# Chunk minimum and maximum by halving steps, and the bounds' product on GpSimd, in a sparse-attention and soft-MoE kernel

## Chip, cores and metric

The kernel runs on one core of a Trainium2 chip. The metric is the device time of one execution in microseconds (us). The engines are TensorE (PE; PEld is its weight load), VectorE (DVE), ScalarE (ACT) and GpSimd (POOL). Each works through its own instructions in program order and waits for others through semaphores. Here POOL also issues every load, and SyncE (SP) issues the stores of the output.

## What is computed

```
# q, k, v: 4 batches x 8 heads x 768 positions x 64, f32
k_min, k_max = min, max of k over each chunk of 32 positions     # 24 chunks
ub   = sum over d of max(q * k_min, q * k_max)                   # bound, per position and chunk
ub   = ub where the chunk is not in the future, else -1e9
top  = the 6 chunks of the largest ub, for each position
attn = softmax(q k^T / 8, over the positions in top, causal) @ v
# soft MoE over x = attn as 3072 rows x 512
logits = x @ phi                                                 # 32 slots
slots  = softmax(logits over rows)^T @ x
y      = relu(slots @ w1[e]) @ w2[e]                             # 8 experts, 4 slots each
out    = softmax(logits over slots) @ y                          # 3072 x 512, f32
```

## The kernel before

The work goes by pairs of heads: 16 pairs, two heads of 64 on the 128 partitions. The program is written out by hand, as a loop `for i in range(-2, 16)` (L469) that is a software pipeline. In round i the scores, the exponentials and the causal masks of pair i are made. For pair i+1 the bounds are made (`ubound`) and the six best chunks are picked (`select`, `ns_transposes`, `evac_ns`). For pair i+2 the keys and queries are transposed and prepared (`transposes`, `evac_T`, `kmin`, `kmax`, `qsplit`). For pair i-1 the product with v is made (`pv`), and pair i-2 is normalised and transposed. The loads of pair i+4 are issued. Four pairs make a batch, so in two of every four rounds MoE steps of a batch come between (`moe_logits` and `moe_copy` in one, `moe_max` to `moe_ct` in the next); the others are plain rounds. Ahead of the loop stands a preamble (L138 to L175): on GpSimd the loads of pairs 0 to 2, of v 0 and 1, of one weight tile and of phi, with mask building between them; on VectorE memsets.

Each engine takes its instructions in the order in which the program issues them, so a step's place in a round is its place in five queues. For GpSimd a round's order is: the masks of scores 0 and 1 (L291, an affine select on e_sb of 128x256), a small cast (L244, into ns_t), the k and q loads (L127), the masks of scores 2 and 3, the v load (L132), a weight load in most rounds (L120), and the masks of scores 4 and 5. For VectorE it is: normalise (inv L320, x_sb L321), the twelve MAX8 (L242), the comparison (ns_t L245), kmin (L202), the copy of xT (L341), kmax (L208) and bd (L210), the copy of nsT (L261), and the two qpn (L218, L219).

The lines that the change touches are these. `kmin` reduces kT (128 x 768, bf16, 24 chunks of 32) to 24 minima, in the tile mm; `kmax` writes the maxima beside them, and then multiplies mm by headsel, a 0/1 mask that keeps each head's rows, into bd (2 x 2 x 24 a partition). In the next round `ubound` reads bd and qpn on TensorE, so that a PSUM tile ub_ps holds the bounds, which MAX8 reads.

The score tiles in PSUM (p_sc) are two, so the scores of a group wait until the exponential two groups before has read its tile. nsT is needed by the mask matmul of the scores (L277). The e_sb tiles are nine.

Of the kernel before, what the change touches and what calls it, by code (L numbers as in the profile page):

```python
# [11 lines left out]
BF16 = mybir.dt.bfloat16  # L12
ALU = mybir.AluOpType
ACT = mybir.ActivationFunctionType
AX = mybir.AxisListType
# [3 lines left out]
CH = 32  # L19
NCHUNK = 24  # L20
NQT = 6
P = 128
# [24 lines left out]
def kernel(  # L47
# [10 lines left out]
    nc = tc.nc  # L58
# [45 lines left out]
    i_ctx, u_ctx, l_ctx = ExitStack(), ExitStack(), ExitStack()  # L104
# [2 lines left out]
    ep = i_ctx.enter_context(tc.tile_pool(name="ep", bufs=9, side="right"))  # L107
    ep5 = i_ctx.enter_context(tc.tile_pool(name="ep5", bufs=2, side="right"))
    tpu = u_ctx.enter_context(tc.tile_pool(name="tpu", bufs=2, side="right"))
    inp = l_ctx.enter_context(tc.tile_pool(name="inp", bufs=3, side="right"))  # L110

    def load_w(i):
# [35 lines left out]
    for h in range(2):  # L148
# [3 lines left out]
        out=qgrp, in_=qgrp, compare_op=ALU.not_equal, fill=1.0, base=0,  # L152
# [3 lines left out]
        out=caus[:4], in_=caus[:4], compare_op=ALU.is_ge, fill=NEG, base=0,  # L156
# [5 lines left out]
    for h in range(2):  # L162
        sl = schunk[h * 64:(h + 1) * 64]
        nc.gpsimd.affine_select(
            out=sl, in_=sl, compare_op=ALU.not_equal, fill=NEG, base=0,
# [3 lines left out]
            out=sl, in_=sl, compare_op=ALU.not_equal, fill=-1.0, base=-NCHUNK,  # L169
# [20 lines left out]
    def evac_T(i, nm):  # L190
# [5 lines left out]
        )  # L196
        st[nm + "T", i] = t

    def kmin(i):
        kT = st["kT", i].rearrange("d (c x) -> d c x", x=CH)  # L200
        mm = tpu.tile([P, 2, 1, NCHUNK], BF16, name="mm", tag="mm")
        nc.vector.tensor_reduce(mm[:, 0, 0, :], kT, axis=AX.X, op=ALU.min)  # L202
        st["mm", i] = mm

    def kmax(i):
        kT = st["kT", i].rearrange("d (c x) -> d c x", x=CH)
        mm = st.pop(("mm", i))
        nc.vector.tensor_reduce(mm[:, 1, 0, :], kT, axis=AX.X, op=ALU.max)  # L208
        bd = tpu.tile([P, 2, 2, NCHUNK], BF16, name="bd", tag="bd")
        nc.vector.tensor_tensor(  # L210
            bd, mm.broadcast_to([P, 2, 2, NCHUNK]), headsel.broadcast_to([P, 2, 2, NCHUNK]), op=ALU.mult,
        )
        st["bd", i] = bd
# [255 lines left out]
    for i in range(-2, NPAIR):  # L469
# [38 lines left out]
        if have(i + 2):  # L508
            transposes(i + 2, "q")
            evac_T(i + 2, "q")  # L510
            kmin(i + 2)
        if have(i - 2):
            evac_x(i - 2)
        if have(i + 2):
            kmax(i + 2)
# [58 lines left out]
    op = ctx.enter_context(tc.tile_pool(name="op", bufs=5))  # L574
# [87 lines left out]
    for m in range(B * NQT // 2):  # L662
        o_sb = op.tile([P, 2, Dm], F32, name="o_sb", tag="o_sb")
        rows = out[m * 2 * P:(m + 1) * 2 * P, :].rearrange("(p x) d -> p x d", x=2)
        for x in range(2):
            pool, tag = homes[n % 5]
# [41 lines left out]
```

## Time and profile before

| | us |
|---|---|
| median of 3 runs (177.87 to 177.99) | 177.93 |
| the profiled execution | 177.53 |
| its span, first to last instruction | 175.8 |
| the reductions L202 and L208, 16 each | 15.2 and 15.1 |
| the products L210, 16 | 4.7 |
| the casts L244 on POOL, 16 | 3.7 |

The span is shorter than the execution, which holds some start and end around it. A timeline line gives the start in the span, the duration, the engine, the line of the source, the operation, the output and input tiles with their sizes, the count, and in brackets the idle time ahead of it with what ended that. The chain of work that ended last is followed back from the last instruction, at each step to what released it; a line gives start, duration and the work. Matmuls overlap in a pipeline, and so do neighbouring VectorE instructions by some 0.08 us where one doesn't need the other, so durations can add up to more than the time between two starts.

### The profile page before, as it was taken

How to read it: one execution, taken by the hardware profiler on the slowest of the kernel's cores; microseconds unless marked ns; L12 is line 12 of the kernel's file. 1: busy time of each engine (PE TensorE's matmuls, PEld its weight loads, DVE VectorE, ACT ScalarE, POOL GpSimd, SP SyncE). 2: the span in 40 equal slices, each digit the busy share in tenths (PEclk: the TensorE clock that was granted, in tenths of full speed). 3: DMA queues.
4: the chain of work that ended last, by engine and by line, in shares of the span. 5: the costliest groups of instructions: out<-in, count | busy, mean ns of one | idle time of the engine just before them, and what ended most of it. 6: DMA issues, size and time to landing. Idle time of an engine off the chain costs nothing.

```text
span 175.8 us, 5994 instructions
## 1 busy us (share of the span) xinstructions
PE 139.1 (79%) x2486; PEld 95.9 (55%) x2486; DVE 128.8 (73%) x429; ACT 120.0 (68%) x163; POOL 99.9 (57%) x194
## 2 busy tenths in 40 slices
PE   0449888999889889999988999999689569986500
PEld 0334556777567657766765776677467444532000
DVE  4456979999889998999998999999752650246530
ACT  2336798989789778988977698897667321156430
POOL 7995679869768557877775585759344600000000
PEclk9999999999999999999999999999999956999755
DMA  3999999999999999999999999199999993009995
GB/s 50 167 158 180 194 206 200 206 197 209 179 212 193 215 185 143 200 172 203 172 147 203 169 207 141 17 187 211 200 214 214 213 215 72 4 13 403 402 405 212
DMA packets 40460, 32.92 MB, mean 187 GB/s; under 512 B 26353, under 2 KB 34545, under 8 KB 40433
## 3 DMA queue, kind: packets, MB, share of 16 engines
q0 software_dynamic: 38416, 26.25, 101.8%
q1 hardware_dynamic: 2016, 6.29, 9.1%
q8 instruction: 19, 0.31, 0.7%
q14 instruction: 9, 0.07, 0.1%
HBM read 52.49 MB, written 6.29 MB: 334 GB/s over the span
## 4 chain that ended last, share of the span: by engine, by line
PE 36%; ACT 19%; DVE 13%; DMA 12%; POOL 11%; issue 5%; POOLq 0%; DVEq 0%; ACTq 0%
ACT e_sb L289 13%; DMA k_in<-in_k_dram 7%; PE sc_ps L271 6%; DMA out_dram<-o_sb 5%; PE at_ps L308 5%; PE sc_ps L277 4%; PE tr_ps L184 3%; PE h_ps L605 3%; DVE x_sb L321 3%; POOL e_sb L291 3%; POOL q_in L127 2%; PE ns_ps L253 2%; POOL k_in L127 2%; PE so_ps L640 2%; PE si_ps L427 2%
## 5 line engine op out<-in xcount | busy, mean ns | idle before, releaser
L289 ACT ACTIVATE e_sb<-sc_ps 128x1024 bf16<-128x1024 f32 x96 | 83.6, 936 | 10.9 <-PE sc_ps L277 9.9
L291 POOL TENSOR_SCALAR_AFFINE_SELECT e_sb<-e_sb 128x256 bf16<-128x256 bf16 x96 | 39.5, 423 | 32.7 <-ACT e_sb L289 32.0
L271 PE MATMUL sc_ps<-qT,kT 64*128 64x512 bf16 (+3 forms) x256 | 39.6, 310 | 6.6 <-ACT e_sb L289 6.3
L277 PE MATMUL sc_ps<-nsT,smask 64*128 64x512 bf16 (+3 forms) x256 | 36.8, 306 | 0.0
L308 PE MATMUL at_ps<-v_t,e_sb 128*128 128x65 bf16 x672 | 29.4, 194 | 1.2 <-DVE x_sb L321 1.1
L308 PEld LDWEIGHTS <-e_sb 128*128 128x128 bf16 x672 | 25.1, 98 | 3.4 <-DVE x_sb L321 1.6
L271 PEld LDWEIGHTS <-kT 64*128 64x128 bf16 x256 | 15.8, 94 | 16.8 <-issue 8.7
L242 DVE MAX8 mx<-ub_ps 128x8 f32<-128x24 f32 x192 | 18.8, 170 | 4.6 <-PE ub_ps L231 4.5
L202 DVE TENSOR_REDUCE mm<-kT 128x24 bf16<-128x768 bf16 x16 | 15.2, 949 | 4.0 <-ACT kT L193 4.0
L132 POOL DMA_DIRECT2D v_t<-in_v_dram x16 | 16.7, 1042 | 1.9 <-PE ns_ps L253 1.2
L193 ACT COPY kT<-tr_ps 128x768 bf16<-128x768 bf16 x16 | 12.8, 803 | 6.5 <-PE tr_ps L184 6.5
L321 DVE TENSOR_TENSOR x_sb<-at_ps,inv 128x768 bf16<-128x768 f32 (+2 forms) x17 | 15.5, 910 | 0.6
L277 PEld LDWEIGHTS <-smask 64*128 64x128 bf16 x256 | 13.1, 95 | 4.4 <-issue 0.3
L208 DVE TENSOR_REDUCE mm<-kT 128x24 bf16<-128x768 bf16 x16 | 15.1, 942 | 0.0
L193 ACT COPY qT<-tr_ps 128x768 bf16<-128x768 bf16 x16 | 13.2, 825 | 2.7 <-PE tr_ps L184 2.7
L184 PE MATMUL tr_ps<-ident,k_in 128*64 128x128 bf16 x192 | 9.2, 237 | 6.6 <-DMA k_in<-in_k_dram 5.5
L670 DVE TENSOR_SCALAR o_sb<-o_ps,cinv 128x512 f32<-128x512 f32 x12 | 8.6, 748 | 7.2 <-PE o_ps L668 4.1
L231 PE MATMUL ub_ps<-bd,qpn 128*128 128x48 bf16 x192 | 10.4, 187 | 2.8 <-DVE qpn L218 2.5
L127 POOL DMA_DIRECT2D k_in<-in_k_dram x16 | 11.7, 729 | 1.3 <-POOLq L692 0.8
L261 DVE COPY nsT<-ns_ps 128x768 bf16<-128x768 bf16 x16 | 8.9, 556 | 4.0 <-PE ns_ps L253 3.5
L672 ACT ACTIVATE o_sb<-o_ps,cinv 128x512 f32<-128x512 f32 x12 | 7.8, 688 | 5.7 <-DMA out_dram<-o_sb 3.8
L127 POOL DMA_DIRECT2D q_in<-in_q_dram x16 | 11.5, 721 | 0.0
(95 smaller groups left out, 213.2 us busy)
## 6 DMA issues: line engine op xcount, KB each, us to landing
w_sb<-in_moe_w_dram POOLq DMA_DIRECT2D x16, 1024.0 KB, 12.9
out_dram<-o_sb SPq DMA_DIRECT2D x10, 512.0 KB, 5.5
k_in<-in_k_dram POOLq DMA_DIRECT2D x16, 192.0 KB, 7.9
q_in<-in_q_dram POOLq DMA_DIRECT2D x16, 192.0 KB, 8.1
v_t<-in_v_dram POOLq DMA_DIRECT2D x16, 192.0 KB, 9.3
out_dram<-o_sb SPq DMA_DIRECT2D x4, 256.0 KB, 3.4
phi_sb<-in_moe_phi_dram POOLq DMA_DIRECT2D x1, 32.0 KB, 9.6
```

The source lines that it names most:

```text
L127: nc.gpsimd.dma_start(out=t, in_=src.rearrange("h (p g) d -> p h (g d)", p=P))
L132: nc.gpsimd.dma_start(out=v_t[i % NV][:, :, :, :D], in_=v[b, 2 * j:2 * j + 2].rearrange("h (g p) d -> p h g d", p=P),)
L193: nc.scalar.copy(t.rearrange("d (p g) -> d p g", g=NQT), st.pop((nm + "ps", i)).rearrange("d g p -> d p g"),)
L202: nc.vector.tensor_reduce(mm[:, 0, 0, :], kT, axis=AX.X, op=ALU.min)
L208: nc.vector.tensor_reduce(mm[:, 1, 0, :], kT, axis=AX.X, op=ALU.max)
L242: nc.vector.max(mx[:, a, :], ub[:, a, :])
L271: nc.tensor.matmul(ps[:, h, c:c + w], lhsT=kT[r, kg * P:(kg + 1) * P], rhs=qT[r, qs], start=True, stop=False,)
L277: nc.tensor.matmul(ps[:, h, c:c + w], lhsT=smask[r, kg].rearrange("p a b -> p (a b)"), rhs=nsT[r, qs], start=False, stop=True,)
L289: nc.scalar.activation(e[:, :, :w], st.pop(("scps", i, g))[:, :, :w], func=ACT.Exp, scale=scale)
L291: nc.gpsimd.affine_select(out=e[:, :, :P], in_=e[:, :, :P], compare_op=ALU.is_ge, fill=0.0, base=0, pattern=[[0, 2], [1, P]], channel_mult ...
L308: nc.tensor.matmul(o, lhsT=st["e", i, g][:, h, c:c + P], rhs=v_t[i % NV][:, h, kg, :], start=(kg == 0), stop=(kg == t),)
L321: nc.vector.tensor_tensor(st["x", b][:, t0:t1, 2 * j:2 * j + 2, :].rearrange("p t h d -> p h t d"), at[:, :, :, :D], inv.broadcast_to([P, ...
```

## The change

The two reductions over 32 elements become three steps each: the elementwise minimum (or maximum) of the first 16 and the last 16 of each chunk, of the first 8 and the last 8 of that, and a reduction over 8. Two tiles of one buffer each, from a new pool, hold what lies between. The product bd goes from VectorE to GpSimd, in the same place of the program.

```diff
+    tpf = u_ctx.enter_context(tc.tile_pool(name="tpf", bufs=1, side="right"))
...
+    def fold(out, kT, op):
+        a = tpf.tile([P, NCHUNK, CH // 2], BF16, name="fold_a", tag="fold_a")
+        nc.vector.tensor_tensor(a, kT[:, :, :CH // 2], kT[:, :, CH // 2:], op=op)
+        b = tpf.tile([P, NCHUNK, CH // 4], BF16, name="fold_b", tag="fold_b")
+        nc.vector.tensor_tensor(b, a[:, :, :CH // 4], a[:, :, CH // 4:], op=op)
+        nc.vector.tensor_reduce(out, b, axis=AX.X, op=op)
+
     def kmin(i):
...
-        nc.vector.tensor_reduce(mm[:, 0, 0, :], kT, axis=AX.X, op=ALU.min)
+        fold(mm[:, 0, 0, :], kT, ALU.min)
         st["mm", i] = mm
 
     def kmax(i):
...
-        nc.vector.tensor_reduce(mm[:, 1, 0, :], kT, axis=AX.X, op=ALU.max)
+        fold(mm[:, 1, 0, :], kT, ALU.max)
         bd = tpu.tile([P, 2, 2, NCHUNK], BF16, name="bd", tag="bd")
-        nc.vector.tensor_tensor(
+        nc.gpsimd.tensor_tensor(
             bd, mm.broadcast_to([P, 2, 2, NCHUNK]), headsel.broadcast_to([P, 2, 2, NCHUNK]), op=ALU.mult,
         )
```

In the built order VectorE has 48 instructions more (two tensor_tensor for each of 32 folds, less 16 products), and GpSimd 16 more; each product stands on GpSimd where it stood in the program, which for pairs 0 and 1 is behind the whole preamble and ahead of the first cast, or behind the loads of round -1. The orders of TensorE and ScalarE are the same.

## The prediction

> **What bounds the kernel now.** I read the page's busy shares first: no engine fills the span.
>
> ```profile
> span 175.8 us, 5994 instructions
> PE 139.1 (79%) x2486; PEld 95.9 (55%) x2486; DVE 128.8 (73%) x429; ACT 120.0 (68%) x163; POOL 99.9 (57%) x194
> ```
>
> So each stage has its own limit, and three stages matter here. Next came the chain that ended last, in order of time; this is its part for the start:
>
> ```profile
> 12.46 0.29 POOL identf masks.py:199
> 13.00 0.83 PE ns_ps L253 x6
> 13.85 0.56 DVE nsT L261
> 14.41 0.86 DVE mm L202
> 15.27 0.87 DVE mm L208
> 16.16 0.26 DVE bd L210
> ```
>
> Up to 12.75 us POOL works through its preamble (loads, masks), and the first work behind it sets the pace. Then VectorE is on the chain, with the very instructions that are changed. The timeline of the same stretch shows why POOL stands there:
>
> ```profile
> 8.46 0.26 DVE L210 TENSOR_TENSOR bd<-mm,headsel 128x96 bf16<-128x96 bf16 x1
> 9.22 0.22 PE L231 MATMUL ub_ps<-bd,qpn 128*128 128x48 bf16 x1 [2.34 <-DVE qpn L218]
> 10.50 1.17 DVE L242 MAX8 mx<-ub_ps 128x8 f32<-128x24 f32 x12 [0.92 <-PE ub_ps L231]
> 12.46 0.29 POOL masks.py:199 TENSOR_SCALAR_AFFINE_SELECT identf<-identf 128x128 f32<-128x128 f32 x1
> 12.71 0.23 POOL L244 CAST ns_t<-mx 128x12 bf16<-128x12 f32 x1
> 13.00 0.82 PE L253 MATMUL ns_ps<-ident,ns_t 128*128 128x128 bf16 x6 [1.75 <-POOL ns_t L244]
> ```
>
> Today bd, the ub matmuls, MAX8 and the comparison of pair 0 (done at 12.17) run beside POOL's preamble. Only the small cast queues behind it.
>
> Third, the timeline of a plain round (no MoE step), 83.46 minus 76.61 = 6.85 us long:
>
> ```profile
> 80.59 0.26 DVE L210 TENSOR_TENSOR bd<-mm,headsel 128x96 bf16<-128x96 bf16 x1
> 81.76 0.39 PE L271 MATMUL sc_ps<-qT,kT 64*128 64x512 bf16 x2 [0.19 <-ACT e_sb L289]
> 82.47 1.94 ACT L289 ACTIVATE e_sb<-sc_ps 128x1024 bf16<-128x1024 f32 x2 [0.48 <-PE sc_ps L277]
> 83.46 1.17 DVE L242 MAX8 mx<-ub_ps 128x8 f32<-128x24 f32 x12 [0.25 <-PE ub_ps L231]
> ```
>
> ScalarE is idle 0.48 us a round, because the next scores wait for a score buffer that its own exponential frees: it closes its own ring of 6.85 us. VectorE's only gap in the round is the 0.25 before MAX8, so it works through 6.6 of the 6.85: room, but little.
>
> **The change, part by part.**
>
> *Start.* In the built order of the changed kernel POOL's preamble stays ahead of the loop, so bd(0) becomes the instruction right behind identf, ahead of the cast. It can't start before 12.71. Its price is in no row: POOL's one-input selects take 0.41 us for 256 elements and 0.29 for 128, so about 0.17 fixed and 0.94 ns an element; 96 elements are 0.26 with one input. Ends: 0.23 (the cast of 12 elements) and 0.53 (two whole one-input passes). I take 0.35 (fixed part once, elements twice). Then bd ends at 13.06, and the ub matmuls start 0.06 later (cast end to ns_ps is that today). From the last wait in ub today (9.64) to MAX8 (10.50) is 0.86; with the two matmuls ahead, MAX8 starts at 14.03. MAX8 to the end of the comparison is 1.67 today (12.17 minus 10.50): 15.70. The cast runs inside that (needs MAX8, 15.2). So ns_ps starts at 15.76 instead of 13.00: **+2.76 us**, since bd, ub, MAX8 and the comparison no longer run beside the preamble but after it.
>
> The Trainium skill ("GPSIMD Engine Reference", section 4.1, Engine selection) speaks against this half of the edit: two-input elementwise work belongs on VectorE, GpSimd being about two times slower. By its 2.6 cycles an element at 1.2 GHz an estimate is 0.21 us for 96 elements, 0.38 with the trace's fixed 0.17, and the sum would grow by 0.03. It speaks of the engine's rate, and nothing of the place in its queue.
>
> *The fold, uncontended.* tensor_reduce: 768 elements 0.945, 192 elements (rm L411) 0.344: 0.144 fixed and 1.04 ns an element. tensor_tensor in f32: 32 elements 0.184, 192 elements 0.358: 0.15 fixed, 1.09 ns an element. Whether bf16 halving runs at two elements a step no row shows for this operation; the bf16 copy L261 does 768 in 0.556, so 0.52 ns an element beside a fixed 0.15, and this nearest row says yes. Then 384 outputs are 0.35, 192 are 0.25, the last reduce 0.34; two dependent starts add 0.04 each (kmax end 80.55, bd 80.59): 1.02 against 0.945, **+0.08** a fold. At one element a step: 0.56 + 0.36 + 0.34 + 0.08 = 1.34, +0.40. At the start two folds of pair 1 are on the chain (+0.16), less bd (0.18 to the next start) = about 0; but bd(1) on POOL comes behind the qpn pair or in between: -0.1 to +0.26. I take **+0.1**.
>
> *Locks in the loop.* These rows decide the rest:
>
> ```profile
> 21.03 0.78 POOL L291 TENSOR_SCALAR_AFFINE_SELECT e_sb<-e_sb 128x256 bf16<-128x256 bf16 x2
> 21.29 0.65 DVE L210 TENSOR_TENSOR bd<-mm,headsel 128x96 bf16<-128x96 bf16 x1
> ...
> 96.84 1.02 POOL L132 DMA_DIRECT2D v_t<-in_v_dram  x1
> 97.60 0.36 DVE L413 TENSOR_TENSOR lc<-lg,rm 128x192 f32<-128x192 f32 x1
> ```
>
> bd takes 0.26 alone and 0.65 under two selects: it ended 0.13 after the second. lc takes its free 0.36 under a DMA issue. So the fold's tensor_tensors will wait for selects, not for issues. qpn does wait for issues: L219 took 0.87 us at 88.50 instead of 0.34, until the v_t issue ended at 89.21.
>
> In a plain round kmin meets the k and q issues (free), kmax meets the selects of scores 2 and 3 (79.56 to 79.99, 80.16 to 80.57). Stepping through: kmax's first half ends at 80.19, its second at 80.71, the reduce at 81.09; nsT starts at 81.04 (80.91 before), ends at 81.60; its first reader, the mask matmul L277, runs at 81.98. Hidden. bd on POOL 81.13 to 81.48; qpn 81.48 to 82.1; x_sb as before: no bd, no late MAX8. **Loop: 0**, with 0.1 to 0.2 us of cover; once it is gone, each excess tenth costs a tenth per round. v_t is issued 0.8 later; behind it stand the w_sb issue and the selects of scores 4 and 5, read a round later, and POOL is level again by the next k issue.
>
> *Given back.* In round 4 the k load comes late:
>
> ```profile
> 45.80 0.53 PE L184 MATMUL tr_ps<-ident,k_in 128*64 128x128 bf16 x12 [0.65 <-DMA k_in<-in_k_dram]
> ```
>
> The round takes 7.80 us by its exponentials (44.26 to 52.06), 0.95 over a plain one. The load was issued 12.5 us earlier into a full queue. All that follows the start moves 2.9 us later, the DMA queue hardly: by 19.9 us 2.87 MB of 3.02 MB issued have moved, so it is not dry when the delayed w_sb 1 comes. The wait goes: **-0.95** (0 to -0.95). In round 1 both qpn waited for issues (0.75 and 0.80 us) on the chain: **-0.3** (0 to -0.4) as v_t comes later.
>
> *Sum.* 177.53 (the profiled execution; its span 175.8 and 1.7 around it) + 2.76 + 0.1 + 0 - 0.95 - 0.3 = 179.14. The median of the runs, 177.93, is 0.40 above the profiled one: **179.5**.
>
> **Rivals.**
>
> *The loop becomes VectorE's* (27%). If v_t's issue takes the port between the two qpn, the second waits as at 88.50: +0.5, 0.4 beyond the cover, in some 8 plain rounds: +3.2, 182.7. For it: 50.88 and 88.02, where v_t began 0.1 to 0.2 ahead of qpn. Against: v_t wants the port 0.39 after its start (1.19 and 1.07 instead of 1.02 fit this), and behind a bd of 0.35 the second qpn is in by then. It decides when bd is shorter than 0.3 us or the folds run 0.2 over my sum. Range 180.4 to 184.
>
> *No doubled rate* (7%). Folds at 1.34: 0.64 more a round, 0.55 beyond the cover, 13 rounds: +7, 186.6. A code load ahead of POOL's first tensor_tensor would land here too; the built order shows none added.
>
> *Not slower* (10%): the loop was VectorE's already, and ScalarE only followed. Then a round loses bd (0.32) and qpn's usual 0.1 of waiting, and pays 0.16: -0.26, times 13 is -3.4 against +1.6: 176.1. VectorE's 6.6 of 6.85 speak for it, ScalarE's wait for its own buffer against. It decides when plain rounds fall under 6.72 us; half as much gives about 178. I split it 7 faster, 3 the same.
>
> *The start partly hidden* (4%): 178.3 to 179.0.
>
> **The numbers.** Forecast 179.5 (179.0 to 180.4): 52%. From 178.3 to 183.2 are the forecast, the partly hidden start and most of the first rival: 8 in 10. The measurement tells 0.2% (0.36 us) from no change: faster 7%, the same 4%, slower 89%.
>
> **What would show it.** bd(0) on POOL at 12.71, ns_ps(0) near 15.8; plain rounds still 6.85; no DMA wait in round 4; kmax's halves stretched under selects; bd on POOL 0.35. I am wrong if ns_ps(0) stays near 13, if plain rounds leave 6.85 by over 0.1, or if the first half takes 0.55 alone.

## The result, and the profile after

The changed kernel takes 178.86 us (177.98 to 180.07), the kernel before, run beside it, 177.18 us (176.21 to 177.99), medians of 17 runs each. The ratio is 1.0105, with a 95% interval of 1.0081 to 1.0129 (it is worked out from the single runs, so it is not quite the quotient of the medians, 1.0095): **slower by about 1%**. The forecast was 179.5 (178.3 to 183.2); 178.86 lies in that range, but just under the 179.0 to 180.4 that the prediction gave to its main path. The profiled execution of the changed kernel took 179.98 us (span 178.2), 2.45 more than that of before; it is among the slowest of its 17, so I use the traces for where the time went, and the medians for how much it is.

Lines below the change stand eight lines lower: the scores are L279 and L285, the masks L299, nsT L269, MAX8 L250. Those above it stand one lower: v_t is L133. The new lines are L202, L204 and L205 (the fold), L218 (bd on POOL), L226 and L227 (qpn). First the busy shares of the page of after:

```profile
span 178.2 us, 6074 instructions
PE 140.3 (79%) x2486; PEld 96.9 (54%) x2486; DVE 125.6 (70%) x477; ACT 119.9 (67%) x163; POOL 105.3 (59%) x210
```

VectorE has 3.2 us less to do, POOL 5.4 more, and the kernel is slower. The shares don't tell that; the start does. This is its part of the chain that ended last, in order of time:

```profile
12.57 0.29 POOL identf masks.py:199
12.86 0.33 POOL bd L218
...
14.11 1.19 DVE mx L250 x12
...
15.92 0.81 PE ns_ps L261 x6
```

ns_ps followed identf's last mask by 0.25 us before. Now bd, the ub matmuls, MAX8 and the comparison of pair 0 stand between, and it starts at 15.92 instead of 13.00: +2.92. The waits of TensorE, by engine, line and releaser (us in total, times, longest), name the new one first:

```profile
PE ub_ps L239 <- POOL bd L218: 5.8, 2, 5.5
...
PE tr_ps L185 <- DMA k_in<-in_k_dram: 4.9, 1, 4.9
```

The first line is the start (5.5 of 5.8). The last shows that of two waits for a k load only the first of all is left; the one of round 4 is gone. A plain round in the timeline of after:

```profile
83.80 0.35 POOL L218 TENSOR_TENSOR bd<-mm,headsel 128x96 bf16<-128x96 bf16 x1 [0.58 <-DVE mm L205]
84.27 1.08 POOL L133 DMA_DIRECT2D v_t<-in_v_dram  x1
84.36 0.35 DVE L227 TENSOR_SCALAR qpn<-qT 128x768 bf16<-128x768 bf16 x1
85.12 1.94 ACT L297 ACTIVATE e_sb<-sc_ps 128x1024 bf16<-128x1024 f32 x2 [0.48 <-PE sc_ps L285]
86.12 1.17 DVE L250 MAX8 mx<-ub_ps 128x8 f32<-128x24 f32 x12 [0.28 <-PE ub_ps L239]
```

ScalarE's gap of 0.48 is as before, and so is the length: its copy of kT starts at 80.09 and at 86.94, 6.85 us apart. The second qpn keeps its 0.35 although the v_t issue begins 0.09 us ahead of it.

To place the difference I set each round's copies of kT and qT on ScalarE (L193, now L194) against those of before. The copy of qT is later by 2.90 us in pair 1, 3.64 in pair 3, 3.33 in pair 4, 2.65 from pair 6 on and some 2.45 from pair 12 on, and the end by 2.45 too. So five steps make the trace's +2.45: **+2.90** at the start, **+0.74** in rounds 0 and 1, **-0.31**, **-0.68** in round 4, **-0.20** in the MoE rounds 9 and 10.

### The profile page after: what moved, and what is told of

Its sections match the earlier page's. It is cut to its first block, busy times and chain, and to the rows that moved or that the text cites. A ratio compares the mean times of both kernels' runs of the same rounds, so it can differ in the third digit from the quotient of the medians.

```text
span 178.2 us, 6074 instructions
## 1 busy us (share of the span) xinstructions
PE 140.3 (79%) x2486; PEld 96.9 (54%) x2486; DVE 125.6 (70%) x477; ACT 119.9 (67%) x163; POOL 105.3 (59%) x210
## 4 chain that ended last, share of the span: by engine, by line
PE 37%; ACT 23%; DVE 17%; POOL 9%; issue 5%; DMA 5%; DVEq 0%; POOLq 0%; ACTq 0%
ACT e_sb L297 17%; PE sc_ps L279 7%; PE at_ps L316 5%; DMA out_dram<-o_sb 5%; PE sc_ps L285 4%; PE tr_ps L185 4%; PE h_ps L613 3%; PE ub_ps L239 3%; DVE x_sb L329 2%; ACT kT L194 2%; PE ns_ps L261 2%; PE so_ps L648 2%; DVE mx L250 2%; POOL e_sb L299 2%; POOL v_t L133 2%
## 5 line engine op out<-in xcount | busy, mean ns | idle before, releaser
L299 POOL TENSOR_SCALAR_AFFINE_SELECT e_sb<-e_sb 128x256 bf16<-128x256 bf16 x96 | 38.5, 419 | 20.6 <-ACT e_sb L297 19.9
L279 PE MATMUL sc_ps<-qT,kT 64*128 64x512 bf16 (+3 forms) x256 | 40.2, 314 | 6.0 <-ACT e_sb L297 5.7
L285 PE MATMUL sc_ps<-nsT,smask 64*128 64x512 bf16 (+3 forms) x256 | 37.3, 311 | 0.0
L316 PE MATMUL at_ps<-v_t,e_sb 128*128 128x65 bf16 x672 | 30.0, 195 | 1.1 <-DVE x_sb L329 1.1
L316 PEld LDWEIGHTS <-e_sb 128*128 128x128 bf16 x672 | 25.6, 99 | 3.2 <-DVE x_sb L329 1.3
L279 PEld LDWEIGHTS <-kT 64*128 64x128 bf16 x256 | 15.8, 95 | 16.6 <-issue 8.6
L250 DVE MAX8 mx<-ub_ps 128x8 f32<-128x24 f32 x192 | 18.7, 170 | 8.7 <-PE ub_ps L239 8.7
L194 ACT COPY kT<-tr_ps 128x768 bf16<-128x768 bf16 x16 | 12.9, 804 | 9.9 <-PE tr_ps L185 9.9
L133 POOL DMA_DIRECT2D v_t<-in_v_dram x16 | 17.3, 1080 | 2.7 <-PE at_ps L316 1.4
L285 PEld LDWEIGHTS <-smask 64*128 64x128 bf16 x256 | 13.2, 96 | 4.6 <-issue 0.5
L194 ACT COPY qT<-tr_ps 128x768 bf16<-128x768 bf16 x16 | 13.2, 827 | 2.9 <-PE tr_ps L185 2.9
L202 DVE TENSOR_TENSOR fold_a<-kT 128x384 bf16<-128x384 bf16 x32 | 12.1, 377 | 3.8 <-ACT kT L194 3.7
L205 DVE TENSOR_REDUCE mm<-fold_b 128x24 bf16<-128x192 bf16 x32 | 11.3, 353 | 2.1
L239 PEld LDWEIGHTS <-qpn 128*128 128x128 bf16 x192 | 8.7, 98 | 6.4 <-issue 4.2
L121 POOL DMA_DIRECT2D w_sb<-in_moe_w_dram x16 | 11.4, 713 | 0.0
```

Of the source, the lines that this page charges most:

```text
L133: nc.gpsimd.dma_start(out=v_t[i % NV][:, :, :, :D], in_=v[b, 2 * j:2 * j + 2].rearrange("h (g p) d -> p h g d", p=P),)
L194: nc.scalar.copy(t.rearrange("d (p g) -> d p g", g=NQT), st.pop((nm + "ps", i)).rearrange("d g p -> d p g"),)
L239: nc.tensor.matmul(ps[:, t, :], lhsT=qpn[:, x, t * P:(t + 1) * P], rhs=bd[:, x].rearrange("p h c -> p (h c)"), start=False, stop=(x == 1),)
L250: nc.vector.max(mx[:, a, :], ub[:, a, :])
L279: nc.tensor.matmul(ps[:, h, c:c + w], lhsT=kT[r, kg * P:(kg + 1) * P], rhs=qT[r, qs], start=True, stop=False,)
L285: nc.tensor.matmul(ps[:, h, c:c + w], lhsT=smask[r, kg].rearrange("p a b -> p (a b)"), rhs=nsT[r, qs], start=False, stop=True,)
```

## The experiments

In all of them the ratio is to the kernel before, run on the same chip (176.82 to 177.09 us). The profiled run of before, 177.53, is 0.4 to 0.7 over those medians, so shifts against its trace come out smaller than differences of medians. My theory was the prediction's: the start is the price, the folds cost nothing in the loop, and round 4 gives some back. The rival was the prediction's first: the loop becomes VectorE's through locks.

**The two halves of the change alone.** `e1_fold_only` keeps `fold` and puts the product back on VectorE:

```diff
-        nc.gpsimd.tensor_tensor(
+        nc.vector.tensor_tensor(
             bd, mm.broadcast_to(...
```

> The product is back on VectorE, the halving steps stay. Theory (the queue place of the first product costs it all): ns_ps of pair 0 starts near 13.0 us again, plain rounds stay 6.85, the wait for the k load in round 4 is back (0.5 to 0.7), and the time is that of the kernel before within 0.5 us (ratio 0.997 to 1.003). Rival A (the folds' longer VectorE time and their waits for selects cost it): start near 13.0 as well, but plain rounds above 6.9 and the time +1 us or more. Rival B (GpSimd's product costs in each round): as the theory here.

It took 178.31 us, 1.0075 [1.0046, 1.0104]: a miss, for I had the folds free. The start and the plain rounds are as before (+0.09 at the start, 6.85 us). The loss comes later: +0.16 and +0.35 after rounds 5 and 6, +0.91 and +1.16 after rounds 9 and 10, where VectorE has the MoE steps as well. The group of the second qpn (total us, mean ns, then idle time) in before, in e1_fold_only and in the change:

```profile
L219 DVE TENSOR_SCALAR qpn<-qT 128x768 bf16<-128x768 bf16 x16 | 7.6, 475 | 0.0
```
```profile
L227 DVE TENSOR_SCALAR qpn<-qT 128x768 bf16<-128x768 bf16 x16 | 9.1, 567 | 0.0
```
```profile
L227 DVE TENSOR_SCALAR qpn<-qT 128x768 bf16<-128x768 bf16 x16 | 7.0, 439 | 0.0
```

It takes 0.35 us when nothing holds it; it is held longest in e1_fold_only, and less in the change than before. Round 9 shows why; its timeline in e1_fold_only:

```profile
86.91 0.91 POOL L299 TENSOR_SCALAR_AFFINE_SELECT e_sb<-e_sb 128x256 bf16<-128x256 bf16 x2
86.98 0.57 DVE L202 TENSOR_TENSOR fold_a<-kT 128x384 bf16<-128x384 bf16 x1
...
88.37 1.03 POOL L133 DMA_DIRECT2D v_t<-in_v_dram  x1 [0.55 <-PE ns_ps L261]
...
89.47 0.81 DVE L227 TENSOR_SCALAR qpn<-qT 128x768 bf16<-128x768 bf16 x1
90.20 0.34 DVE L371 COPY lg<-lg_ps 128x192 f32<-128x192 f32 x1
```

and in the change:

```profile
91.21 0.35 DVE L227 TENSOR_SCALAR qpn<-qT 128x768 bf16<-128x768 bf16 x1
91.66 1.07 POOL L133 DMA_DIRECT2D v_t<-in_v_dram  x1 [0.66 <-PE at_ps L316]
91.70 0.36 DVE L371 COPY lg<-lg_ps 128x192 f32<-128x192 f32 x1
```

VectorE works without a gap from the first reduction of this round to the logits' copy lg, so every tenth counts. Before, that took 4.16 us (85.13 to 89.29); e1_fold_only takes 4.63 (85.57 to 90.20): +0.08 in kmin's fold, +0.39 in kmax's under two selects, -0.14 at bd, +0.14 at the two qpn under the v_t issue. The change takes 3.92 (87.78 to 91.70): the folds and the absent bd together cost +0.07, but the two qpn take 0.31 less, since v_t is issued after them.

`e2_product_only` keeps the reductions over 32 and moves the product:

```diff
-        nc.vector.tensor_tensor(
+        nc.gpsimd.tensor_tensor(
             bd, mm.broadcast_to(...
```

> The reductions over 32 are back, the product stays on GpSimd. Theory: ns_ps of pair 0 near 15.9, no wait for the k load in round 4, time +1.4 to +2.4 us over the kernel before, like the whole change. Rival A: within 0.5 us of the kernel before. Rival B: +1.4 to +2.4 too, but spread over the rounds.

179.38 us, 1.0136 [1.0102, 1.0170], more than the whole change, and 2.44 us over the kernel before, where I had expected at most 2.4. The start shift is there (kT of pair 1 at 15.02, +3.73; from the next pair on +2.45), ns_ps starts at 16.04, and 0.95 of that has come back by the end of round 4. In plain rounds the second qpn is held nearly always:

```profile
45.20 1.18 POOL L132 DMA_DIRECT2D v_t<-in_v_dram  x1
...
45.66 0.88 DVE L219 TENSOR_SCALAR qpn<-qT 128x768 bf16<-128x768 bf16 x1
```

Its mean is 0.679 us, its median 0.875; but the plain rounds stay 6.85, so such a lock is covered there, in a kernel whose VectorE has no bd to make. The halves cost 1.37 and 2.44 us by medians, together 1.68: they are not additive. With both, folds and product meet POOL's instructions at other times.

**The first product alone.** `e3_pair0_on_vector` is the change, with only bd(0) left on VectorE:

```diff
-        nc.gpsimd.tensor_tensor(
+        (nc.vector if i == 0 else nc.gpsimd).tensor_tensor(
             bd, mm.broadcast_to(...
```

> The whole change, but the product of pair 0 alone stays on VectorE; the other 15 are on GpSimd. Theory: ns_ps of pair 0 near 13.0, the time of the kernel before within 0.6 us. Rival A and rival B: ns_ps near 13.0, yet +1 us or more over the kernel before, since 15 of 16 products and all folds are as in the change.

**176.15 us, 0.9951 [0.9921, 0.9980]**: faster than both kernels, and by 0.79 us of medians, more than the 0.6 that I had allowed. ns_ps(0) is back:

```profile
13.07 0.82 PE L261 MATMUL ns_ps<-ident,ns_t 128*128 128x128 bf16 x6 [1.76 <-POOL ns_t L252]
```

`g4_first_product_only` is the mirror of it, the kernel before with bd(0) alone on POOL:

```diff
-        nc.vector.tensor_tensor(
+        (nc.gpsimd if i == 0 else nc.vector).tensor_tensor(
             bd, mm.broadcast_to(...
```

> The kernel before, with pair 0's product alone on GpSimd; the 15 other products and all reductions as before. Theory: the place of one 0.35 us instruction in GpSimd's queue at the start is the price of the change: ns_ps(0) at 15.8 to 16.1 us, every round 2.8 to 3.0 us later, of which 0.7 to 0.95 come back as the k wait of round 4 goes; the time is 1.4 to 2.4 us over the kernel before. Rival: the other 15 products carry part of the cost; then this kernel is under 0.7 us slower.

179.57 us, 1.0170 [1.0132, 1.0208]: 2.75 us slower by medians, and 1.46 by the profiled executions. The rival (under 0.7) is out; the median lies over my range of 1.4 to 2.4, the trace at its lower end.

```profile
12.76 0.34 POOL L210 TENSOR_TENSOR bd<-mm,headsel 128x96 bf16<-128x96 bf16 x1
...
15.84 0.80 PE L253 MATMUL ns_ps<-ident,ns_t 128*128 128x128 bf16 x6 [1.07 <-DVE ns_t L245]
```

These two runs settle the cause. One instruction of 0.34 us behind POOL's preamble costs 1.7%; all the rest of the change gains 0.5%; 1.0170 times 0.9951 is 1.0120, inside the interval of the change. The single traces don't add up so well: +1.46 and -0.58 against +2.45.

**Another order of the preamble.** `e4_preamble_tail_later` is the change with the tail of POOL's preamble moved behind kmax:

```diff
-    load_v(0)
-    load_v(1)
-    nc.gpsimd.dma_start(out=phi_sb, in_=moe_phi.rearrange(...))
-    make_identity(nc, identf)
...
+        if i == -1:
+            load_v(0)
+            load_v(1)
...
+        if i == 0:
+            nc.gpsimd.dma_start(out=phi_sb, in_=moe_phi.rearrange(...))
+            make_identity(nc, identf)
```

> The whole change, but four pieces of GpSimd's preamble move behind the first product: the v loads of pairs 0 and 1 go to the end of round -1's maximum step, phi's load and the f32 identity to round 0. Theory: the first product starts at about 9.5, behind the schunk selects, and ns_ps of pair 0 near 12.4, 0.6 ahead of the kernel before. Since the loads' bandwidth, not the start, then sets when the k load of round 4 lands, the wait there is back and longer (1 to 1.4 us), and the time is that of the kernel before, -0.6 to +0.4 us. If nothing were given back in round 4, -0.6 to -1. Rivals A and B: still +1 us or more above the kernel before.

177.16 us, 0.9998 [0.9974, 1.0023], as expected. The change's loss is gone although bd(0) is on POOL: what cost was its place in the queue, and not the engine. It runs at 9.57, and ns_ps(0) starts at 12.66, 0.34 us ahead of before (0.6 expected). But what e3_pair0_on_vector gained is missing. Its timeline has a wait in round 4 (k load of that round), longer than the 0.65 of before, and from there to pair 11 the trace is 0.86 us later than before:

```profile
46.66 0.53 PE L181 MATMUL tr_ps<-ident,k_in 128*64 128x128 bf16 x12 [0.99 <-DMA k_in<-in_k_dram]
```

**Is the extra 0.74 of rounds 0 and 1 a cold TensorE?** A cold TensorE here means one that takes 0.85 us for twelve transposes, a warm one takes 0.53. In round 0 of the change the transposes of k and q of pair 2 take 0.85 us each time (20.69 and 23.29), against 0.71 and 0.53 before. `f1_change_warm` is the change, with twelve unused matmuls of 512 columns ahead of ub(0):

```diff
+            nc.tensor.matmul(
+                ps[:, 0, :], lhsT=ident, rhs=c_pad...[:, :512], start=True, stop=True,
+            )
```

> The whole change, with 12 matmuls of 512 columns, whose result nothing reads, on TensorE ahead of the bounds of pair 0, where it waits for the first product from 6.7 to 13.1 us. Theory (a part of the change's loss is that TensorE, idle for so long, runs its first rounds at half pace: 12 transposes take 0.85 us at 23.29, where the kernel before has 0.53 from 18.4 on): the transposes of pair 1 take 0.53 at 14, ns_ps 0.51, the start up to round 1 comes 0.5 to 1.2 us earlier than in the change, and the time is 0.3 to 1.0 us under that of the change (which is 1.7 over the kernel before). Rival (the pace of these matmuls has another cause): the same 0.85 and the change's time.

178.50 us, 1.0067 [1.0031, 1.0103]; the interval overlaps that of the change, so a gain isn't shown. The matmuls run from 7.24 to 12.11; the transposes of k of pairs 1 and 2 after them:

```profile
13.76 0.53 PE L185 MATMUL tr_ps<-ident,k_in 128*64 128x128 bf16 x12
...
20.46 0.85 PE L185 MATMUL tr_ps<-ident,k_in 128*64 128x128 bf16 x12
```

0.53, and then 0.85 again, already for q of pair 1 (16.41): TensorE was warm and is cold at the next transposes, so twelve matmuls once don't cure it. The gaps of the start fit this; that they are the cause was only argued. The granted clock of the page doesn't show this.

Other runs tell against the change as the cause. `f2_weights_later` and `g1_weights_moved` (both below) have the instructions of before in round 0. In f2_weights_later the warm pace comes at 20.4 instead of 18.2; in g1_weights_moved the transposes of pair 2 are as slow as in the change. And in g4_first_product_only, where the first product is as late as in the change, they are warm. Their transposes of k of pair 2, g1_weights_moved first:

```profile
17.94 0.85 PE L184 MATMUL tr_ps<-ident,k_in 128*64 128x128 bf16 x12
```
```profile
20.35 0.53 PE L184 MATMUL tr_ps<-ident,k_in 128*64 128x128 bf16 x12
```

The copies of qT of pair 2 are 0.40 us (f2_weights_later) and 0.59 us (g1_weights_moved) later than in the trace of before. So executions of the same instructions differ here by as much as the transposes cost the change, some 0.45 us, and this part isn't shown to be the change's. Over all runs the warm pace came between 17 and 25 us.

**What is the wait of round 4 worth?** `f2_weights_later` is the kernel before, with the weight load of round 1 given to round 11:

```diff
-    for i in (2, 5, 8, 11):
+    for i in (1, 2, 5, 8):
         wplan[i] = 0
```

> The kernel before, with the weight load of round 1 left out there and made in round 11 (same number of loads). Theory (what the change got back in round 4 is a wait for bandwidth: the k load of pair 6 stands behind that weight load): no wait for the k load in round 4, that round 6.85 instead of 7.80, the time 0.5 to 1.1 us under the kernel before. Rival (the wait is latency or the issue on GpSimd): round 4 stays near 7.8 and the time the same.

176.93 us, 1.0001 [0.9976, 1.0025]: a miss in time. The wait is gone and the trace 0.56 us earlier from round 5 on, but the medians show nothing. `f3_tail_weights_later` puts the same on e4_preamble_tail_later:

> The whole change with the preamble's tail later (as in e4) and the weight load of round 1 moved to round 11. Theory: the wait in round 4 of e4 (0.99 us and a second one in the round) goes, and the time is 1.0 to 1.8 us under e4, so 0.8 to 1.8 us under the kernel before. Rival (in e4 something else than the loads holds round 4): e4's time.

176.50 us, 0.9979 [0.9946, 1.0012]: not told apart from before, 0.59 us by medians where at least 0.8 was expected, though its trace is 0.86 us earlier. `f4_all` adds eight unused matmuls to that:

> f3 with idle-time matmuls on TensorE as in f1, 3 ahead of the first transposes and 5 ahead of the bounds of pair 0. Theory: 0.3 to 1.0 us under f3, 1.2 to 2.6 us under the kernel before. Rival: as f3, or slower by the matmuls' own time where they hold the bounds back (up to 0.4 us).

176.29 us, 0.9961 [0.9932, 0.9989]: a small gain, but 0.80 us by medians, where at least 1.2 was expected, and 0.21 under f3_tail_weights_later. Its trace is 1.57 us earlier in the last pairs and 1.69 at the end. Its chain goes through the last weight load:

```profile
127.63 22.26 DMA w_sb<-in_moe_w_dram
```

So I moved the loads otherwise in `g1_weights_moved`. (That this load ended f2_weights_later too, as I then supposed, its own chain doesn't show: no weight load stands on it behind 100 us.)

```diff
-    for i in (2, 5, 8, 11):
+    for i in (1, 5, 8):
         wplan[i] = 0
-    for i in (12, 13):
-        wplan[i] = 2
+    wplan[12] = 2
```

> The kernel before, with two weight loads moved: the load of round 1 goes to round 2, behind the k load of pair 6, and one of round 13's two goes to round 11, where the DMA engines stand idle. Theory: f2_weights_later took the k wait out of round 4 (its trace came 0.56 us earlier from round 5 on) but gained nothing in the medians, because the last weight load then ended the kernel; with the last load earlier as well, round 4 is a plain 6.85 us, and the time is 0.5 to 1.1 us under the kernel before (ratio 0.994 to 0.997). Rival: the round-4 wait isn't worth anything at the end, and the ratio is 1.000 as that of f2_weights_later.

176.60 us, 0.9995 [0.9967, 1.0023]: the rival's answer. Its trace is 0.34 earlier. It has no wait for the k load in round 4. So what the wait of round 4 is worth in this kernel is too little for these medians to show, with intervals of 0.25 to 0.3% either way.

**Is the loss of the folds alone the v_t issue?** `g3_fold_v_later` is e1_fold_only with the v and weight loads issued behind the masks of scores 4 and 5:

```diff
-        if have(i + 2) and i >= 0:
-            load_v(i + 2)
-        if i < EARLY:
-            weights(i)
...
             scores(i, 5)
             expo(i, 5)
+        if have(i + 2) and i >= 0:
+            load_v(i + 2)
+        if i < EARLY:
+            weights(i)
```

> e1_fold_only (the halving steps, the product on VectorE as before), with the v load and the weight loads of each round issued after the selects of scores 4 and 5. Theory: e1_fold_only loses in the mixture-of-experts rounds because folds and product push the two head-mask products into the issue of the v load, which held the second at a median of 0.56 us; with the issue later the second has a median near 0.35 us, and the time is within 0.4 us of the kernel before, against +1.3 for e1_fold_only. Rival: the folds' own time on VectorE (about 0.3 us a round more than the two reductions) is what it loses; then it stays at +1 us or more.

180.72 us, 1.0229 [1.0187, 1.0271], 3.9 us over the kernel before. The theory's 0.4 is out, and the rival's "+1 us or more" is met, but the run doesn't separate the two, since it takes no lock away: the masks move forward to where the issue was and hold the same instructions.

```profile
83.34 0.88 POOL L299 TENSOR_SCALAR_AFFINE_SELECT e_sb<-e_sb 128x256 bf16<-128x256 bf16 x2 [1.13 <-ACT e_sb L297]
83.38 0.58 DVE L226 TENSOR_SCALAR qpn<-qT 128x768 bf16<-128x768 bf16 x1
```

The second qpn of that round, at 83.88, takes 0.55 too; over all rounds it has a median of 0.55 us, not the 0.35 I expected, and v_t is issued only behind them, at 84.17. Of e1_fold_only's loss, the split read off round 9 stands; that it holds for every round was not tried.

**The gains together.** `g2_best` is the change with bd(0) on VectorE, e4's preamble and g1's loads.

> The change, with pair 0's product on VectorE, the loads of v_0 and v_1 and two constants put behind pair 0's extremes, and the weight loads as in g1_weights_moved. Theory: the change loses only in its start (the first product behind GpSimd's start work), and what it gains in round 4 and in the mixture-of-experts rounds stays: 1 to 2 us under the kernel before (ratio 0.989 to 0.995). Rival: the gains overlap with those of e3_pair0_on_vector, and the ratio is 0.995 again.

**175.68 us, 0.9936 [0.9908, 0.9965]**, the fastest kernel here, faster than before and than the change. Its interval overlaps that of e3_pair0_on_vector, so what it adds to that isn't shown.

## Why the prediction was right, point by point

*The start, +2.76.* Right in mechanism and nearly in size: +2.92 at ns_ps, +2.90 at the next copy. bd(0) ran at 12.84, not at 12.71, and MAX8 started at 14.11 (predicted 14.03); g4_first_product_only and e3_pair0_on_vector show that this one step is the price.

*bd on POOL, 0.35.* Measured 0.34 in the start, mean 0.347. The Trainium skill ("GPSIMD Engine Reference", section 3.1, Elementwise, with 2.6 cycles an element) led to an estimate of 0.38; the measurement decides for the two-input price from the trace's rows. Neither price is the loss: the place in the queue cost 2.9 us.

*The fold, 0.35, 0.25 and 0.34.* Right. Uncontended they take 0.35, 0.26 and 0.35; this group has the means with the locks:

```profile
L202 DVE TENSOR_TENSOR fold_a<-kT 128x384 bf16<-128x384 bf16 x32 | 12.1, 377 | 3.8 <-ACT kT L194 3.7
...
L204 DVE TENSOR_TENSOR fold_b<-fold_a 128x192 bf16<-128x192 bf16 x32 | 10.3, 323 | 1.1
```

The halving does run at two elements a step: 0.36 us for 384 outputs, where one element a step had given 0.56. So the rival with no doubled rate is out.

*bd(1) and the first rounds, +0.1.* Right for what it counted: bd(1) ran with the second qpn (19.29 and 19.38) and held it at 0.50, but the transposes of pair 2 then start 2.92 us late, after 2.90 in the round before. What the sum left out came behind that, +0.74 in rounds 0 and 1. The transposes ran cold, 0.14 and 0.32 longer, which isn't shown to be the change's doing (above). And in round 0 the first qpn met the v_t issue for 0.95 us, against 0.53 before (the second meets the weight issue in both, 0.80 and 0.78):

```profile
25.49 1.08 POOL L133 DMA_DIRECT2D v_t<-in_v_dram  x1
25.78 0.95 DVE L226 TENSOR_SCALAR qpn<-qT 128x768 bf16<-128x768 bf16 x1
```

*The qpn of round 1, -0.3.* Right: they take 0.35 each (at 32.84 and 33.11) instead of 0.75 and 0.80, and ScalarE's copies gain 0.31.

*The loop, 0.* Right for plain rounds (6.85 exactly). In the MoE rounds, which I had not stepped through, the change gains 0.2, and the folds without the moved product lose over 1 us. The rival of the locks was right that they occur (e1_fold_only, e2_product_only), but not in the change: there v_t's issue begins only 0.08 to 0.10 us ahead of the second qpn of a plain round, and the qpn keeps its 0.35, as the prediction argued against the rival. Its price isn't borne out either: it put such a lock at 0.4 us a plain round, and the plain rounds of e2_product_only, which has no folds, stay 6.85 with it.

*Round 4, -0.95.* Mis-sized: -0.68. The wait is gone, but the round takes 7.09 us by its exponentials, not 6.85; it takes 7.09 in g4_first_product_only and e3_pair0_on_vector as well. I had measured it by a plain round. In e3_pair0_on_vector, which is only 0.35 us late ahead of it, the wait goes too: it didn't need 2.9.

*Sum.* Predicted +1.61, found +2.45 between the profiled executions and +1.68 between the medians. Of the traces' sum, +0.64 (first rounds) and +0.27 (round 4) were missing and the start was 0.14 short; -0.20 (the MoE rounds) was missing too. So the mechanism and the size of the start were right, but that the sum met the medians within 0.1 us is partly luck. The 0.40 that I had added from profile to median did not hold for the new runs (before 177.18, under its profiled 177.53), so the time came out 0.64 under the forecast. By its number alone 178.86 falls to the rival of a partly hidden start (178.3 to 179.0), which did not happen: the start cost its full 2.9.

Why executions of one kernel differ by 1% stays open; the traces show two places. One is the pace of the transposes at the start. The other is the end: behind the last copy of kT the change has 60.1 us of span and f1_change_warm, with the same instructions there, 58.5, and in the 5 us that begin 30 us behind that copy the granted clocks are 0.77 and 0.98. The trace of e4_preamble_tail_later, 0.68 us later than before in the last pair, ends 0.60 earlier. So a shift of some tenths in one trace isn't yet a difference between kernels.

## What to carry to other kernels

Before an instruction goes to another engine, look at what stands ahead of it in that engine's queue in the first rounds, not only at its duration and the steady state: here one 0.34 us instruction of sixteen cost more than the whole edit gained, and leaving that one where it was turned +1% into -0.5%. Where two engines lock each other, two edits are not the sum of their parts; step through the rounds with the most work on the shared engine, not through the plain ones. A late load that is waited for once can be worth less than its wait: without the 0.65 us of round 4 the medians moved by nothing that could be told apart.

## What the runs showed of the hardware

A tensor_tensor with both inputs in SBUF runs free beside the issue of a load and waits for a select on POOL: in the change and e1_fold_only a fold_a of kmin takes 0.35 to 0.38 us under the k and q issues, that of kmax mostly 0.45 to 0.59 under the selects of scores 2 and 3. The Trainium skill ("SBUF — State Buffer", section Who interferes with whom) has this as an inference, that a tensor_tensor takes only the read side of the shared port, which the issue doesn't need; these rows agree.

The v_t issue doesn't block from its first moment: a qpn that starts 0.26 us after it (33.11 in the change) keeps its 0.35, and the issue takes 1.24 instead of 1.02; one that starts 0.29 after it (25.78 in the change) takes 0.95, and one 0.46 after it (e2_product_only) 0.88.

TensorE's pace at the start is not visible in the granted clock: the page shows 9 there (1.00 from 0 to 28 us) while twelve transposes take 0.85 us, and 0.53 later. The Trainium skill ("TensorE: Matmul & The Clock Gate", Part 1) says that a free-running window of activity decides, and that the count of cold matmuls varies from run to run; the warm pace at 18.2 us (before) and 20.4 (f2_weights_later) with the same instructions agrees.
